# Loads of the attention sent at the entries into TensorE's instruction blocks

## The chip, the cores and the metric

One Trainium2 chip, one core of it. A core has five engines that run their own instruction streams: TensorE (PE, with its weight loads as PEld), VectorE (DVE), ScalarE (ACT), GpSimd (POOL) and SyncE (SP, which here only starts transfers), and 16 DMA engines. The metric is the device time of one execution in microseconds. The kernel before took 863.31 us (median of three runs, 861.24 to 863.8).

## The reference

Band attention with global rows, then two MLPs over the same tokens.

```
attention, 4 batches x 8 heads, 32 global + 512 local tokens, head size 64:
  out_g = softmax(q_g k_all / 8) v_all                    # global rows see everything
  out_l = softmax([q_l k_g, q_l k_l if |i-j| <= 32] / 8) [v_g, v_l]
x = out as (4 * 544, 512)
x = elu(x @ w_in) @ w_out              # 512 -> 2048 -> 512
h = x @ w2_in;  g = h if h >= 1, 0 if h <= -1, else (h + 1)^2 / 4
return g @ w2_out
```

All in float32; products in the MLPs are made of a high and a low part of each factor, three matmuls for one.

## The kernel before, in words

The attention comes first. Two heads share a tile (a pair; 16 pairs), and the stage runs over 24 units, in groups of three: the local rows of a pair, the global rows of that pair and the next, the local rows of the next pair. Iteration n of the loop (L732) does the scores of unit n (`s` or `sg`), the transposes of the probabilities of unit n-1 (`pt`, `tg`), the output transposes of unit n-2 (`ot`, `tg3`) and the products with v of unit n-1 (`po`, `pog`). From n = 4 on the first weights are split between them (`prep`, six half tiles of raw words, `wraw`), from n = 9 on the first matmuls of the MLP (`up`) are mixed in. About 125 us after the start the MLPs follow (`up` and `dn`), TensorE going from matmul to matmul.

In the attention the instruction order of each engine is the order of the program (`Pinned`). SP's order is its queue: a load that waits holds up all loads behind it. Loads are issued in `arrive(n)` at the end of an iteration. Each pair needs q (272 KB), k (288 KB) and two halves of v (520 KB each), each half tile of words 512 KB. `load` paces v and words: a load waits until all but the newest 3200 words for each partition have landed (`IN_FLIGHT`). q and k have two buffers each, v has six halves, the raw words one. After k has landed GpSimd spreads it (`spread_keys`), and makes small diagonal tiles of q for the global rows (`spread_queries`).

Of the kernel before, what the change touches and what calls it, by code (L numbers as in the profile page):

```python
# [9 lines left out]
F32 = mybir.dt.float32  # L10
# [11 lines left out]
S = SG + SL  # L22
# [3 lines left out]
P = 128  # L26
NPAIR = H // 2
# [26 lines left out]

V_UNTIL = {0: 2, 1: 4, 2: 6, 3: 7, 4: 9, 5: 11}

# [10 lines left out]
def band_attention_then_two_mlps(  # L67
# [35 lines left out]
    acc = {}  # L103

    class Pinned:


        def __init__(self, engine):
            self.engine = engine

        def __getattr__(self, name):
            fn = getattr(self.engine, name)
            return lambda *args, **kw: tc.keep_in_program_order(fn(*args, **kw))  # L113

# [10 lines left out]

    def load(out, src, words, paced=True):
# [12 lines left out]
        loads.append((ins, words))  # L139
# [21 lines left out]

    def prep(wraw_p, wtmp_p, layer, f, c0, n, raw_tag="wraw"):

# [7 lines left out]
        raw = wraw_p.tile([P, n], U64, tag=raw_tag, name="wraw")  # L171
        load(raw, (w1, w2)[layer][f][:, c0:c0 + n], 2 * n)
        words = raw.bitcast(U32).rearrange("p (n two) -> p n two", two=2)
# [203 lines left out]
    with ExitStack() as actx:  # L377
# [6 lines left out]
        sp_p = apool("sp", 4, side="right")  # L384
        raw_p = apool("raw", 2, side="right")
        win_p = apool("win", 4, side="right")
# [20 lines left out]

        def load_qk(b, hp):
            q_sb = raw_p.tile([P, S], F32, tag="q", name="q_sb")
            k_sb = raw_p.tile([P, KPAD + NSUB * 64], F32, tag="k", name="k_sb")  # L410
            both = [(q_sb, qT), (k_sb[:, 0:KPAD], kT)]
            for sb, dram in both if b + hp else both[::-1]:
                load(sb, dram[b, hp], sb.shape[1], paced=False)
            loaded[b, hp] = [q_sb, k_sb, diag[(NPAIR * b + hp) % 4]]

        def load_v(b, hp, es=(0, 1)):
            for e in es:
                v_sb = win_p.tile([P, 2, half * VW + 2], F32, tag="v", name="v_sb", bufs=6)
                v_sb = v_sb[:, :, 0:half * VW]
                src = vwin[b, hp, :, half * e:half * e + half]  # L420
                src = src.rearrange("p (s a) h v -> p s (a h v)", s=2)
                load(v_sb, src, half * 2 * VW)
                v_sb = v_sb.rearrange("p s (a h v) -> p s a h v", a=half // 2, h=2)
                landed.setdefault((b, hp), []).append(v_sb)
# [233 lines left out]
        for _ in range(WARM_UP):  # L658
            eng.tensor.matmul(idle, zeros[:, 0:P], zeros)
        load_qk(*pairs[0])  # L660
        eng.scalar.dma_start(mask_sb, mask)
        eng.scalar.dma_start(eye_sb, eye)
        load_qk(*pairs[1])
        load_v(*pairs[0])
# [11 lines left out]
        def early_weights():  # L676

            for part in parts:
                for _ in range(3):
                    next(part, None)  # L680
                    yield
# [17 lines left out]

        parts = [prep(g_p, wtmp_p, 0, *part, raw_tag="wraw") for part in halves]  # L700
        sent = iter(parts)
        weights, ups = early_weights(), early_ups()
# [7 lines left out]

        def arrive(n):
# [19 lines left out]
        live, first = {}, {}  # L731
        for n in range(len(units) + 2):  # L732
            if n > UP_AT:
                next(ups, None)
            part(n, "scores")
            part(n - 2, "norm")
            part(n - 1, "turn")
# [12 lines left out]
            arrive(n)  # L750
            if n == len(units):
# [144 lines left out]
```

## Time and profile before

| | |
|---|---|
| median of three runs | 863.31 us |
| profiled execution, its own time | 864.74 us |
| its span, first to last instruction | 862.9 us |
| PE, DVE, ACT busy | 844.9, 581.4, 431.7 us |
| mean granted TensorE clock | 0.996 |
| attention stage, to the first `dn` | about 129 us |

Times in the views are microseconds from the span's start. A wait in brackets is idle time just before the row, and what ended it; "issue" means that the profile shows nothing that the engine waited for. The queue q1 carries the loads, q8 the instructions of TensorE. A share of the DMA is the mean busy share of the 16 DMA engines.

### The profile page before, as it was taken

How to read it: one execution, taken by the hardware profiler on the slowest of the kernel's cores; microseconds unless marked ns; L12 is line 12 of the kernel's file. 1: busy time of each engine (PE TensorE's matmuls, PEld its weight loads, DVE VectorE, ACT ScalarE, POOL GpSimd, SP SyncE). 2: the span in 40 equal slices, each digit the busy share in tenths (PEclk: the TensorE clock that was granted, in tenths of full speed). 3: DMA queues.
4: the chain of work that ended last, by engine and by line, in shares of the span. 5: the costliest groups of instructions: out<-in, count | busy, mean ns of one | idle time of the engine just before them, and what ended most of it. 6: DMA issues, size and time to landing. Idle time of an engine off the chain costs nothing.

```text
span 862.9 us, 14906 instructions
## 1 busy us (share of the span) xinstructions
PE 844.9 (98%) x6138; PEld 694.0 (80%) x6138; DVE 581.4 (67%) x1130; ACT 431.7 (50%) x755; POOL 28.2 (3%) x66
## 2 busy tenths in 40 slices
PE   8799899999999999999999999999999999999998
PEld 5677778888888888888888888888888888888886
DVE  4689765879527964834399896368759754845455
ACT  5678674666335543533357564456435333433332
POOL 2122200000000000000000000000000000000000
PEclk9999999999999999999999999999999999999999
DMA  8888722222101210200022112012101200000014
GB/s 265 288 275 266 222 78 98 97 98 98 50 0 49 98 49 0 98 1 1 0 71 77 49 50 97 1 40 93 63 1 58 90 0 1 1 1 0 2 62 146
DMA packets 23124, 65.45 MB, mean 76 GB/s; under 512 B 3984, under 2 KB 4240, under 8 KB 19344
## 3 DMA queue, kind: packets, MB, share of 16 engines
q1 hardware_dynamic: 22768, 64.23, 21.8%
q8 instruction: 48, 0.79, 0.4%
q10 hardware_dynamic: 288, 0.26, 0.1%
q14 instruction: 20, 0.16, 0.1%
HBM read 60.03 MB, written 4.46 MB: 75 GB/s over the span
## 4 chain that ended last, share of the span: by engine, by line
PE 93%; DMA 3%; DVE 2%; issue 1%; ACT 1%; SPq 0%
PE dn L320 40%; PE up L247 39%; PE up L244 3%; PE dn L337 3%; PE up L113 2%; PE po L113 2%; DMA k_sb<-in_kT 1%; PE pt L113 1%; PE s L113 1%; PE sg L113 1%; PE tg L113 1%; DMA wraw<-in_w 1%; DVE top L113 1%; DMA v_sb<-in_vwin 1%; PE ot L113 1%
## 5 line engine op out<-in xcount | busy, mean ns | idle before, releaser
L320 PE MATMUL dn<-gh,wh 128*128 128x512 f32 x506 | 196.9, 389 | 0.0
L320 PE MATMUL dn<-gl,wh 128*128 128x512 f32 x506 | 196.8, 389 | 0.0
L320 PE MATMUL dn<-gh,wl 128*128 128x512 f32 x506 | 196.3, 390 | 0.0
L247 PE MATMUL up<-xh,wl 128*128 128x512 f32 x492 | 192.5, 391 | 0.0
L247 PE MATMUL up<-xl,wh 128*128 128x512 f32 x492 | 191.6, 389 | 0.0
L247 PE MATMUL up<-xh,wh 128*128 128x512 f32 x492 | 191.6, 389 | 0.0
L278 ACT ACTIVATE gh<-g 128x512 fp32r<-128x512 f32 x123 | 77.7, 632 | 118.7 <-DVE g L267 71.8
L297 DVE TENSOR_TENSOR acc<-dn,acc 128x512 f32<-128x512 f32 x128 | 84.9, 685 | 48.7 <-PE dn L320 48.4
L320 PEld LDWEIGHTS dn<-gl,wh 128*128 128x128 f32 x506 | 95.0, 188 | 19.9
L282 DVE TENSOR_TENSOR gl<-g,gh 128x512 fp32r<-128x512 f32 x123 | 84.6, 689 | 38.9 <-ACT gh L278 37.8
L320 PEld LDWEIGHTS dn<-gh,wh 128*128 128x128 f32 x506 | 95.0, 188 | 19.4
L320 PEld LDWEIGHTS dn<-gh,wl 128*128 128x128 f32 x506 | 95.0, 188 | 19.4
L247 PEld LDWEIGHTS up<-xh,wh 128*128 128x128 f32 x492 | 92.3, 188 | 19.3
L247 PEld LDWEIGHTS up<-xl,wh 128*128 128x128 f32 x492 | 92.4, 188 | 18.8
L247 PEld LDWEIGHTS up<-xh,wl 128*128 128x128 f32 x492 | 92.4, 188 | 18.7
L258 ACT ACTIVATE g<-up,half_sb 128x512 f32<-128x512 f32 (+1 forms) x69 | 47.0, 681 | 113.6 <-PE up L247 104.8
L266 DVE SCALAR_TENSOR_TENSOR g<-g 128x512 f32<-128x512 f32 (+1 forms) x69 | 46.9, 680 | 59.4 <-ACT g L258 59.3
L264 DVE SCALAR_TENSOR_TENSOR g<-up,g 128x512 f32<-128x512 f32 x64 | 43.4, 679 | 62.5 <-ACT g L255 62.5
L253 ACT ACTIVATE g<-up 128x512 f32<-128x512 f32 x64 | 37.8, 590 | 86.2 <-PE up L247 80.6
L267 DVE TENSOR_TENSOR g<-g,e 128x512 f32<-128x512 f32 (+1 forms) x69 | 46.9, 680 | 3.6
L180 ACT ACTIVATE top<-wraw 128x1024 f32<-128x1024 f32 x29 | 33.7, 1163 | 29.2 <-DMA wraw<-in_w 24.1
L255 ACT ACTIVATE g<-g,one_sb 128x512 f32<-128x512 f32 x64 | 45.8, 716 | 1.8
(112 smaller groups left out, 923.6 us busy)
## 6 DMA issues: line engine op xcount, KB each, us to landing
wraw<-in_w SPq DMA_DIRECT2D x29, 1024.0 KB, 4.8
v_sb<-in_vwin SPq DMA_DIRECT2D x32, 520.0 KB, 5.3
k_sb<-in_kT SPq DMA_DIRECT2D x16, 288.0 KB, 3.9
q_sb<-in_qT SPq DMA_DIRECT2D x16, 272.0 KB, 5.2
outT<-acc SPq DMA_DIRECT2D x16, 256.0 KB, 2.1
wraw<-in_w SPq DMA_DIRECT2D x6, 512.0 KB, 4.6
outT<-acc_rows SPq DMA_DIRECT2D x4, 64.0 KB, 2.2
mask_sb<-in_mask ACTq DMA_DIRECT2D x1, 192.0 KB, 3.4
```

What stands on the lines that cost most here:

```text
L113: return lambda *args, **kw: tc.keep_in_program_order(fn(*args, **kw))
L247: eng.tensor.matmul(self.ps, w, x, start=k == 0, stop=k == 3 * KT - 1)
L253: eng.scalar.activation(self.g, self.ps, AF.Exp)
L255: eng.scalar.activation(self.g, self.g, AF.Relu, bias=one_sb, scale=-1.0)
L258: eng.scalar.activation(self.g, self.ps, AF.Relu, bias=half_sb, scale=0.5)
L264: eng.vector.scalar_tensor_tensor(g, self.ps, 0.0, g, ALU.max, ALU.subtract)
L266: eng.vector.scalar_tensor_tensor(g, g, 1.0, g, ALU.min, ALU.mult)
L267: eng.vector.tensor_tensor(g, g, self.e, ALU.add)
L278: eng.scalar.activation(self.gh, self.g, AF.Copy)
L282: eng.vector.tensor_tensor(self.gl, self.g, self.gh.bitcast(F32), ALU.subtract)
L297: eng.vector.tensor_tensor(a, ps, a, ALU.add)
L320: eng.tensor.matmul(banks[d], w[:, d * P:(d + 1) * P], g, start=f == fs[0] and k == 0, stop=f == fs[-1] and k == 2,)
```

## The change

Loads from the third pair's q and k and the second pair's v on are no longer issued where the program's loop comes by. The wrapper of TensorE counts what it issues, 4 for a matmul of float32 and 2 for another matmul or a transpose, and when the count passes 186 + 250.5 k it calls `by_blocks` with that matmul. That picks up to three items (q and k of a pair, a half of v, a half tile of words), in the order in which they will be needed, as far as buffers allow, and each waits for that matmul to be done. The pacing by words in flight doesn't apply to these v loads; for the words `load` still has it. q and k have three buffers; the third k lies in the accumulator of the MLP's first batch, which the attention doesn't use.

```
+AT_ONCE = 3
+FIRST_BLOCK, BLOCK = 186, 250.5
...
+            def issue(*args, **kw):
+                ins = tc.keep_in_program_order(fn(*args, **kw))
+                if name in ("matmul", "transpose"):
+                    self.issued += 4 if name == "matmul" and args[1].dtype == F32 else 2
+                    if self.issued > FIRST_BLOCK + self.block * BLOCK:
+                        self.block += 1
+                        at_block(ins)
+                return ins
...
+    def load(out, src, words, paced=True, behind=None):
         ins = eng.sync.dma_start(out, src)
+        if behind is not None:
+            tc.add_manual_dep(ins.ins, behind.ins.name, LANDED, reason="loads by blocks")
...
+        qs = [raw_p.tile([P, S], F32, name=f"q_sb{i}") for i in range(3)]
+        ks = [raw_p.tile([P, k_cols], F32, name=f"k_sb{i}") for i in range(2)]
+        ks.append(acc[0].rearrange("p d n -> p (d n)")[:, 0:k_cols])
...
+        def by_blocks(ins):
+            for _ in range(AT_ONCE):
+                found = []
+                p = now["qk"]
+                if p < len(pairs) and now["n"] >= 3 * ((p - 3) // 2) + 1 + (p - 3) % 2:
+                    found.append((3 * (p // 2) + p % 2 - 1, 0, send_qk))
+                p = len(pairs) - (len(ahead) + 1) // 2
+                if ahead and 2 * len(pairs) - len(ahead) < now["until"]:
+                    found.append((3 * (p // 2) + p % 2 + 1, 1, send_v))
+                if now["free"] and len(parts) < len(halves):
+                    found.append((3 * len(parts) + 3, 2, send_words))
+                if found:
+                    min(found, key=lambda item: item[:2])[2](ins)
...
-            if r == 1 and p + 1 < len(pairs):
-                load_qk(*pairs[p + 1])
-            elif r == 2 and p + 2 < len(pairs):
-                load_qk(*pairs[p + 2])
-            elif r == 0 and g:
-                next(next(sent, iter([0])))
-            while ahead and len(ahead) > 2 * len(pairs) - V_UNTIL.get(n, 4 * g + (4, 6, 7)[r]):
-                load_v(*ahead.pop(0))
+            now["until"] = 4 * g + (6, 6, 8)[r]
+            while now["qk"] < len(pairs) and now["qk"] <= p + (r == 2):
+                send_qk()
...
+            if n > 3 and n % 3 == 2:
+                now["free"] = True
```

SP's queue at the start of the attention, first as it was, from the third pair's q on; the numbers of buffers tell loads apart, DMAHW are semaphores of earlier loads.

```order
L113 DMA q_sb_286<-in_qT 128x544 [waits DMAHW0_49,DMAHW1_49,PE_49,Pool_49]
L113 DMA k_sb_287<-in_kT 128x576 [waits DVE_49,PE_49,Activation_49]
L113 DMA v_sb_290<-in_vwin 128x2x520 [waits DMAHW6_49,DMAHW2_49]
L113 DMA v_sb_292<-in_vwin 128x2x520 [waits DMAHW7_49,DMAHW3_49]
L113 DMA q_sb_398<-in_qT 128x544 [waits DMAHW4_49,PE_49,Pool_49]
L113 DMA k_sb_399<-in_kT 128x576 [waits DMAHW5_49,Pool_49]
L113 DMA v_sb_402<-in_vwin 128x2x520 [waits DMAHW2_49]
L113 DMA v_sb_404<-in_vwin 128x2x520 [waits DMAHW3_49]
L113 DMA wraw_519<-in_w1 128x512 [waits DMAHW5_49,DMAHW0_49]
```

The same loads on SP in the changed kernel. The first row and the fifth begin a burst: they wait for a matmul (PE), and the others stand behind them in the queue.

```order
L126 DMA q_sb2_127<-in_qT 128x544 [waits DMAHW0_49,PE_49]
L126 DMA acc0_90<-in_kT 128x576 [waits DMAHW1_49]
L126 DMA v_sb_244<-in_vwin 128x2x520 [waits DMAHW2_49]
L126 DMA v_sb_246<-in_vwin 128x2x520 [waits DMAHW3_49]
L126 DMA q_sb0_125<-in_qT 128x544 [waits DMAHW4_49,PE_49,Pool_49]
L126 DMA k_sb0_128<-in_kT 128x576 [waits DMAHW5_49,DVE_49,Activation_49]
L126 DMA wraw_330<-in_w1 128x512 [waits DMAHW6_49,DMAHW2_49]
L126 DMA v_sb_335<-in_vwin 128x2x520 [waits DMAHW7_49]
L126 DMA v_sb_442<-in_vwin 128x2x520 [waits DMAHW0_49,PE_49]
```

The first words move ahead of the third pair's v, and each burst has one wait for TensorE at its head where every load had waits of its own. Later, in the repeating part of the stage, SP has this order now (from the eighth pair on):

```order
L113 DMA q_sb_1275<-in_qT 128x544
L113 DMA k_sb_1276<-in_kT 128x576
L113 DMA v_sb_1279<-in_vwin 128x2x520
L113 DMA v_sb_1281<-in_vwin 128x2x520
L113 DMA q_sb_1394<-in_qT 128x544
L113 DMA k_sb_1395<-in_kT 128x576
L113 DMA v_sb_1398<-in_vwin 128x2x520
L113 DMA wraw_1525<-in_w1 128x512
L113 DMA v_sb_1530<-in_vwin 128x2x520
```

And in the changed kernel, one group's three bursts, of 1600, 1592 and 520 KB:

```order
L126 DMA q_sb0_125<-in_qT 128x544
L126 DMA k_sb0_128<-in_kT 128x576
L126 DMA v_sb_1276<-in_vwin 128x2x520
L126 DMA v_sb_1278<-in_vwin 128x2x520
L126 DMA wraw_1391<-in_w1 128x512
L126 DMA q_sb1_126<-in_qT 128x544
L126 DMA k_sb1_129<-in_kT 128x576
L126 DMA v_sb_1398<-in_vwin 128x2x520
L126 DMA v_sb_1510<-in_vwin 128x2x520
```

The words head the second burst, ahead of q and k; the third holds a half of v alone. TensorE's order is the same in both kernels but for the names of the buffers.

## Rows read from the trace of the kernel before

**Rows 1.** The page: engines' busy time; the instruction queue (packets, MB, share).

```profile
PE 844.9 (98%) x6138; PEld 694.0 (80%) x6138; DVE 581.4 (67%) x1130; ACT 431.7 (50%) x755; POOL 28.2 (3%) x66
...
q8 instruction: 48, 0.79, 0.4%
```

**Rows 2.** Waits of TensorE: us in total, times, longest us.

```profile
PE s L113 <- issue: 2.8, 3, 1.8
PE pog L113 <- issue: 2.7, 2, 1.4
...
PE po L113 <- issue: 2.4, 2, 1.9
...
PE sg L113 <- DMA k_sb<-in_kT: 0.4, 1, 0.4
...
PE pog L113 <- DMA v_sb<-in_vwin: 0.2, 1, 0.2
```

**Rows 3.** Timeline of TensorE: start, us, what, count, idle before.

```profile
10.14 1.09 PE L113 MATMUL pt<-eye_sb,sn 128*128 128x128 f32 x8
...
16.36 1.21 PE L113 MATMUL pog<-v_sb,pgT 96*32 96x65 f32 x48
...
19.96 1.16 PE L113 MATMUL po<-v_sb,pT 128*32 128x65 f32 x64
21.05 1.22 PE L113 MATMUL sg<-k_sb,diag 128*64 128x272 f32 x12
...
29.97 0.65 PE L113 MATMUL pog<-v_sb,pgT 96*32 96x65 f32 x14 [1.26 <-issue]
...
33.82 0.42 PE L113 MATMUL po<-v_sb,pT 128*32 128x65 f32 x13
36.15 1.32 PE L113 MATMUL po<-v_sb,pT 128*32 128x65 f32 x51 [1.90 <-issue]
37.39 2.19 PE L113 MATMUL sg<-k_sb,diag 128*64 128x272 f32 x12
```

**Rows 4.** DMA, from 29.97 to 33.7 us, then 33.7 to 34.8.

```profile
q1 hardware_dynamic: 607, 1.21, 93.4%
...
q8 instruction: 1, 0.02, 5.8%
```

**Rows 5.** TensorE at 117.57, and DMA from 118 to 119.5 (tenths in 40 slices).

```profile
117.57 0.39 PE L113 MATMUL up<-xh,wl 128*128 128x512 f32 x1
...
DMA  0009000000000000000000000000000000000000
```

**Rows 6.** Windows: busy us (instructions) of PE, PEld, DVE, ACT, POOL; PEclk, DMA share, GB/s.

```profile
25.00:30.00 5.00, 3.38 (x126) 2.55 (x115) 4.70 (x24) 3.43 (x9) 1.14 (x2) 1.00 0.96 313
...
35.00:40.00 5.00, 3.85 (x66) 2.96 (x66) 2.57 (x6) 2.21 (x7) 1.20 (x2) 0.66 0.80 235
...
90.00:95.00 5.00, 4.72 (x104) 3.75 (x111) 2.79 (x18) 2.51 (x7) 0.42 (x2) 0.66 0.41 119
```

**Rows 7.** Windows by groups of three units: n = 3 to 5, 6 to 8, 12 to 14.

```profile
17.49:31.39 13.90, 11.62 (x357) 9.19 (x350) 11.25 (x53) 12.21 (x35) 3.56 (x8) 1.00 0.92 301
31.39:48.35 16.96, 13.25 (x358) 10.17 (x351) 12.00 (x55) 10.49 (x29) 3.21 (x8) 0.90 0.87 279
62.00:76.69 14.69, 13.99 (x368) 11.10 (x363) 13.38 (x57) 12.34 (x33) 3.73 (x8) 1.00 0.82 262
```

**Rows 8.** The tile q_sb from 90 to 93 us: one load and its matmuls.

```profile
L113 PE MATMUL s<-k_sb,q_sb x38: 266/269/293, 90.3 to 90.9; 64*32 64x128 f32 x38
...
L113 SPq DMA_DIRECT2D q_sb<-in_qT x1: 341/341/341, 91.2 to 91.2; - x1
...
DMA to landing us min/median/max: 2.9/2.9/2.9
```

**Rows 9.** Timeline of SP from 5 to 12 us.

```profile
7.04 0.34 SPq L113 DMA_DIRECT2D q_sb<-in_qT  x1
...
10.40 1.62 SPq L113 DMA_DIRECT2D v_sb<-in_vwin  x2
```

More of the change, by code (lines that the diff above doesn't have):

```diff
@@ L103, in band_attention_then_two_mlps, with at_block @@
     acc = {}
+    on_block = []
+    def at_block(ins):
+        for what in on_block:
+            what(ins)
     class Pinned:
@@ L109, in __init__ @@
             self.engine = engine
+            self.issued = 0
+            self.block = 0
         def __getattr__(self, name):
             fn = getattr(self.engine, name)
-            return lambda *args, **kw: tc.keep_in_program_order(fn(*args, **kw))
+            def issue(*args, **kw):
[6 more added lines that the diff above has]
+                return ins
+            return issue
     class Engines:
@@ L160, in place, with prep @@
         return ring[ci % 2], f - chunks[ci][1][0]
-    def prep(wraw_p, wtmp_p, layer, f, c0, n, raw_tag="wraw"):
+    def prep(wraw_p, wtmp_p, layer, f, c0, n, raw_tag="wraw", behind=None):
         tiles, at = place(layer, f)
@@ L171, in prep @@
         raw = wraw_p.tile([P, n], U64, tag=raw_tag, name="wraw")
-        load(raw, (w1, w2)[layer][f][:, c0:c0 + n], 2 * n)
+        load(raw, (w1, w2)[layer][f][:, c0:c0 + n], 2 * n, behind=behind)
         words = raw.bitcast(U32).rearrange("p (n two) -> p n two", two=2)
@@ L384, in band_attention_then_two_mlps @@
         sp_p = apool("sp", 4, side="right")
-        raw_p = apool("raw", 2, side="right")
+        raw_p = apool("raw", 1, side="right")
         win_p = apool("win", 4, side="right")
@@ L406, in band_attention_then_two_mlps, with load_qk, load_v @@
         half = NSUB // 2
-        def load_qk(b, hp):
-            q_sb = raw_p.tile([P, S], F32, tag="q", name="q_sb")
-            k_sb = raw_p.tile([P, KPAD + NSUB * 64], F32, tag="k", name="k_sb")
+        k_cols = KPAD + NSUB * 64
+        qs = [raw_p.tile([P, S], F32, name=f"q_sb{i}") for i in range(3)]
+        ks = [raw_p.tile([P, k_cols], F32, name=f"k_sb{i}") for i in range(2)]
+        ks.append(acc[0].rearrange("p d n -> p (d n)")[:, 0:k_cols])
+        def load_qk(p, behind=None):
+            b, hp = pairs[p]
+            q_sb, k_sb = qs[p % 3], ks[p % 3]
             both = [(q_sb, qT), (k_sb[:, 0:KPAD], kT)]
[L412 to L416, printed above, removed]
+            for sb, dram in both if p else both[::-1]:
+                load(sb, dram[b, hp], sb.shape[1], paced=False, behind=behind)
+            loaded[b, hp] = [q_sb, k_sb, diag[p % 4]]
+        def load_v(b, hp, es=(0, 1), behind=None):
             for e in es:
@@ L421, in load_v @@
                 src = src.rearrange("p (s a) h v -> p s (a h v)", s=2)
-                load(v_sb, src, half * 2 * VW)
+                load(v_sb, src, half * 2 * VW, paced=behind is None, behind=behind)
                 v_sb = v_sb.rearrange("p s (a h v) -> p s a h v", a=half // 2, h=2)
@@ L659, in band_attention_then_two_mlps @@
             eng.tensor.matmul(idle, zeros[:, 0:P], zeros)
-        load_qk(*pairs[0])
+        load_qk(0)
         eng.scalar.dma_start(mask_sb, mask)
         eng.scalar.dma_start(eye_sb, eye)
-        load_qk(*pairs[1])
+        load_qk(1)
         load_v(*pairs[0])
@@ L676, in early_weights @@
         def early_weights():
-            for part in parts:
+            for i in range(len(halves)):
+                while len(parts) <= i:
+                    send_words()
                 for _ in range(3):
-                    next(part, None)
+                    next(parts[i], None)
                     yield
@@ L698, in early_ups @@
                 u.low()
-        parts = [prep(g_p, wtmp_p, 0, *part, raw_tag="wraw") for part in halves]
-        sent = iter(parts)
+        parts, now = [], dict(n=0, until=4, free=True, qk=2)
         weights, ups = early_weights(), early_ups()
@@ L709, in part, with send_qk, send_v, send_words @@
                 live[n][name]()
-        def arrive(n):
+        def send_qk(behind=None):
+            load_qk(now["qk"], behind)
+            now["qk"] += 1
+        def send_v(behind=None):
+            load_v(*ahead.pop(0), behind=behind)
+        def send_words(behind=None):
+            parts.append(prep(g_p, wtmp_p, 0, *halves[len(parts)], behind=behind))
+            next(parts[-1])
+            now["free"] = False
+        def by_blocks(ins):
[11 more added lines that the diff above has]
+                    min(found, key=lambda item: item[:2])[2](ins)
+        def arrive(n, place):
             g, r = divmod(n, 3)
             p = 2 * g + 1
-            if r == 1 and p + 1 < len(pairs):
-                load_qk(*pairs[p + 1])
-            elif r == 2 and p + 2 < len(pairs):
-                load_qk(*pairs[p + 2])
-            elif r == 0 and g:
-                next(next(sent, iter([0])))
-            while ahead and len(ahead) > 2 * len(pairs) - V_UNTIL.get(n, 4 * g + (4, 6, 7)[r]):
-                load_v(*ahead.pop(0))
+            now["n"] = n
+            if place == 0:
+                return
+            now["until"] = 4 * g + (6, 6, 8)[r]
+            while now["qk"] < len(pairs) and now["qk"] <= p + (r == 2):
+                send_qk()
             if r == 0 and g and p < len(pairs):
@@ L731, in band_attention_then_two_mlps @@
         live, first = {}, {}
+        on_block.append(by_blocks)
         for n in range(len(units) + 2):
@@ L735, in band_attention_then_two_mlps @@
             part(n, "scores")
+            arrive(n, 0)
             part(n - 2, "norm")
@@ L748, in band_attention_then_two_mlps @@
             part(n - 1, "values")
-            arrive(n)
+            arrive(n, 1)
             if n == len(units):
```

2 lines of the change are left out of this document (removed).

## The prediction

> **What bounds the kernel now.** I read the page's busy row first: TensorE is busy for 98% of the 862.9 us span [rows 1]. So a change to loads can only win what TensorE loses, and the view to ask next is its waits. Nearly all of them lie in the first 125 us, the attention stage: 7.9 us, in seven waits, go to "issue", which is time in which TensorE waited for nothing that the profile shows; the data loads stopped it for 0.6 us in all [rows 2]. The timeline shows where the issue waits stand: inside a run of equal matmuls, for instance between record 13 and record 51 of one `po` [rows 3]. Counting records between two of them gives a multiple of 125 each time (36 `pog` from 29.97 us on, 64 `s`, 8 `pt`, 4 `tg`, 13 `po` to the next), and 125 records are 250 of the change's units. 48 instruction packets serve 6138 matmuls and as many weight loads [rows 1], 256 instructions each. So these are entries into blocks of instructions that have not arrived.
>
> Next the DMA view in two narrow windows [rows 4]. TensorE entered a block at 29.97 us. Until 33.7 us no instruction packet ran, though the data queue kept its 16 engines 93% busy; then one packet ran within 1.1 us, and TensorE went on at 36.15 [rows 3]. The fetch for the block after is thus due when a block is entered; it stood 3.7 us behind data, took about 1.0 (5.8% of 16 engines in 1.1 us), and 1.4 us later the block could start. By the same count a block is entered at the `up` of 117.57 us; no data moved then, and the packet ran in the fourth fortieth of the window from 118.0, some 0.6 us after the entry [rows 5]. An undisturbed fetch therefore needs about 0.8 + 1.0 + 1.4 = 3.2 us; blocks here last 2.6 to 8 us.
>
> The clock says what the longest stalls cost besides: after the 1.90 and the 1.82 us waits TensorE was granted 0.66 on the mean of the 5 us window, part of it at 1.2 GHz instead of 2.4 [rows 6]. `sg` x12 took 2.19 us there against 1.22 at 21.05, and the 51 `po` before it 1.32 where 51 x 0.017 are 0.87 [rows 3]: 1.4 us, and the second place alike, 2.8 us together.
>
> **The change, part by part.** It removes the pacing and makes each load wait for the first matmul of a block, up to three items at once (q and k of a pair count as one). The engines' instruction order is the same but for SP and the buffers' names, so TensorE's work is untouched.
>
> What could go: 7.9 us of issue waits. Each is counted from the modelled end of the last matmul, which lies about 0.2 us after its successor would have begun (13 `po` take 0.42 us on their own, where 64 take 1.16, or 0.017 for each further one [rows 3]), so seven stalls cost 7.9 + 7 x 0.2 = 9.3. With the clock: 12.1 us.
>
> What comes back as fetch stalls: this is the largest unknown, and I work it out block by block. With the stalls taken out, the blocks from the first entry (the last of eight `pt` begun at 10.14 [rows 3], at 10.96 us) on last 2.6, 3.7, 5.6, 3.8, 4.1, 4.4, 4.1, 4.5, 6.1, 3.9, 4.9, 6.1, 3.8, 5.0, 6.1, 3.6, 5.8, 4.9, 3.6 us; three make one group of three units, and 3.9 + 4.9 + 6.1 fits the 14.69 us of such a group [rows 7]. SP started a load at 91.24, 0.4 us after the last matmul it waited for [rows 8], and that load of 272 KB, alone in the queue, landed 2.9 us after [rows 8]. At the full rate (313 GB/s at a share of 0.96, so 326 [rows 6]) its bytes take 0.85, so a burst's bytes flow from about 2.0 us behind the entry. The bursts, in KB: 1600, 1592, 1600, 1600, 1592, then 1040, 1600, 1072, 1040, and then the repeating 1600, 1592, 520. A full one takes 5.0 us, so it ends 7.0 us behind its entry, later than all blocks but one end. The rule I carry from block to block: the fetch starts 0.8 us after its entry or when the bursts of earlier blocks are through, whichever is later; the next block starts 2.4 us after that, or when the matmuls are done. It gives stalls of 0.6, 0.2, 0, 0.6, 1.0, 0.55, 0, 0.8 in the first eight blocks, then 0.65 once in each group of three, and 1.45 at the nineteenth: 6.5 us. None reaches 1.8, so I cost the clock at nothing. The same rule with 313 GB/s gives 8.8 and with 340 gives 4.6 (single windows go from 294, 235 at a share of 0.80 [rows 6], to 347, 1.21 MB in 3.73 us at 0.934 [rows 4]); I keep 326, the busiest window's.
>
> What is late at the start: now the third pair's q goes out at 7.04 us and the second pair's v at 10.40 [rows 9]. Afterwards these and k wait for the first block entry, so q starts at 11.4 and its bytes at 13.0; 560 KB and then two v halves of 520 end at 14.8, 16.4 and 18.1, and land some 0.45 later. Global rows of the first two heads' pairs (`pog`, 16.36 us now [rows 3]) would be ready at 15.85, wait 1.0 us for the first half of v, and, 0.6 us of work later, 1.1 for the second: 2.1 us. A bound from the other side is 0.5, if the bytes start with the 10.40 rows' delay; nothing below, since no load is earlier. Behind these matmuls stand all of TensorE's later ones. Word loads come earlier than now, which hides them fully; they do wait for VectorE to release the one word buffer, and the loads behind that word load on SP then start up to 1.5 us late. I cost that at nothing, since most bursts find the queue still full; without that cover it is one more stall of up to 1.5.
>
> What VectorE keeps: in the group from 17.49 us on VectorE is busy for 11.25 us and ScalarE for 12.21, TensorE for 11.62, and in the next VectorE for 12.00 [rows 7]. Without stalls these groups cannot be shorter than 12.2 and 12.0 us, where TensorE would come to some 11.7 each; they keep 0.8 us of the gain. The third buffers for q and k and the k buffer laid into the accumulator add no instruction; the accumulator's first real write comes after the attention.
>
> Sum: -12.1 + 6.5 + 2.1 + 0.8 = -2.7 us, against the profiled execution's 864.74 (span 862.9 and 1.8 around it), so 862.0. That execution is 0.17% above the median of 863.31; set against the median the forecast is **860.6 us**.
>
> **Rivals.** *First, the fetch finds the way free.* Bursts issued back to back may move at 347 GB/s or more, and every entry that finds the engines empty has its fetch before the new data. For it: the 340 case already leaves only 4.6, and the DMA share of a late group is 0.82 [rows 7]. Against it: the early groups need 3.8 MB in 12 us. Stalls of 3, `pog` late by 1.5 and VectorE's 0.8 give 5.3 - 12.1 = -6.8, so 856.5.
> A rule speaks for this side. The Trainium skill (DMA: Bandwidth & Descriptors, Queues, rings and completion order) says that a DMA engine takes turns between its queues packet by packet; by that a fetch waits for about one packet, and only the first entry's 0.6 would be left, some 854.7. The trace disagrees: 3.7 us with no instruction packet among 607 of data [rows 4]; so I give it no more than this rival's chance.
>
> *Second, on the other side: the burst's first load overtakes the fetch.* It holds if a busy DMA engine serves in order of arrival and the load's descriptors get there first: SP needs 0.4 + 0.34 us to have issued it, the fetch is seen 0.6 us after its entry at best. Then each fetch due in a busy queue also waits for a load of 272 to 520 KB, 0.85 to 1.6 us, and the same rule gives 15.3 us of stalls, four of them over 2 us. Time 15.3 + 2.1 + 0.8 - 12.1 = +6.1, so 869.4. For it: how closely those times lie together. Against it: the fetch has a lead of some 0.6 us over the first bytes. It decides from the point where first bytes flow less than about 1 us after an entry.
>
> *Third, the stalls only move.* At 300 to 313 GB/s the rule leaves 8.8 or more, and every stall over 1.8 would bring the slow clock back: -12.1 + 8.8 + 2.1 + 0.8 = -0.4, so 862.9. The same time comes out if the change does not do what it says because its count of units drifts from the true entries: loads then go out at fixed but arbitrary places, and stalls stay as frequent.
>
> **Chances.** Forecast 0.43 (its own range 858 to 863), free way 0.16, overtaking 0.20, stalls that move 0.21. A measurement of this kernel tells a change from none at about 0.3%, 2.6 us. The forecast lies just at that edge: some 0.25 of its 0.43 is faster, 0.17 the same, 0.01 slower; free way is all faster; moved stalls are the same but for 0.03 slower; overtaking is slower but for 0.01. Faster 0.41, same 0.36, slower 0.23. The range from 855.5 to 868.5 leaves out the far end of the free way and half of the overtaking.
>
> **What would show it.** Right: issue waits of 5 to 8 us, more of them (eight to twelve) and none over 1.5; no granted clock under 1.0 before 125 us; a wait of `pog` for v_sb of 1 to 2 us near 16 us; stage end (the first `dn`) some 3 us earlier. Wrong: issue waits over 10 us, or several over 1.8 with the clock at 1.2 GHz behind them (overtaking); under 4 us (free way); new waits of TensorE for k_sb or POOL after 20 us, which I have at zero; or a change in the span after 130 us, which nothing here touches.

## The result, and the profile after

The changed kernel takes 867.6 us (median of 7, 866.65 to 871.55) where the kernel before takes 862.98 on the same chip: 1.0061 of it, 95% interval 1.0043 to 1.0080. It is slower by 0.6%; the prediction, 860.6 us, had the wrong sign, though its wide range (855.5 to 868.5) still holds 867.6. The profiled execution took 867.51 us (span 865.7), 2.8 more than that of before.

TensorE's waits after, in the columns of [rows 2]:

```profile
PE tg L126 <- DVE og L126: 3.9, 5, 0.8
PE po L126 <- issue: 3.8, 4, 1.8
PE pog L126 <- DMA v_sb<-in_vwin: 3.0, 2, 2.1
...
PE pt L126 <- ACT wh L126: 0.7, 1, 0.7
PE pog L126 <- issue: 0.6, 1, 0.6
PE po L126 <- DMA v_sb<-in_vwin: 0.5, 1, 0.5
...
PE s L126 <- issue: 0.2, 1, 0.2
```

The issue waits fell from 7.9 us to 4.6; the waits for `v_sb` rose from 0.2 to 3.5, and those of `tg` for VectorE's `og` from 2.5 to 3.9. The waits for v come at the start, where the timeline of after (start, us, what, count, idle before) has:

```profile
14.65 0.30 PE L126 MATMUL pog<-v_sb,pgT 96*32 96x65 f32 x2
15.85 0.77 PE L126 MATMUL pog<-v_sb,pgT 96*32 96x65 f32 x24 [0.90 <-DMA v_sb<-in_vwin]
18.76 1.02 PE L126 MATMUL pog<-v_sb,pgT 64*32 64x65 f32 x22 [2.15 <-DMA v_sb<-in_vwin]
19.72 1.96 PE L126 MATMUL s<-acc,q_sb 64*32 64x128 f32 x64
21.60 1.97 PE L126 MATMUL pt<-eye_sb,sn 128*128 128x128 f32 x8
23.50 0.48 PE L126 MATMUL tg<-eye_sb,og 128*64 128x64 f32 x4
23.92 1.75 PE L126 MATMUL po<-v_sb,pT 128*32 128x65 f32 x64
...
33.85 1.16 PE L126 MATMUL s<-k_sb,q_sb 64*32 64x128 f32 x64
```

The 48 `pog` that ran in one piece before [rows 3] wait twice, 3.05 us. And then the same 64 `s` take 1.96 us that take 1.16 at 33.85; 8 `pt` take 1.97 where 1.09 was the duration before, 64 `po` 1.75 for 1.16 [rows 3]. The windows of after, in the columns of [rows 6], show the clock that goes with it:

```profile
15.00:20.00 5.00, 2.00 (x62) 1.40 (x70) 0.99 (x4) 2.67 (x9) 1.52 (x6) 0.85 1.00 345
20.00:25.00 5.00, 5.00 (x116) 4.17 (x104) 2.40 (x20) 1.99 (x6) 1.24 (x3) 0.50 0.70 233
25.00:30.00 5.00, 4.83 (x138) 3.98 (x136) 2.92 (x8) 4.20 (x12) 1.69 (x4) 0.97 0.64 214
...
45.00:50.00 5.00, 4.33 (x166) 3.45 (x171) 4.58 (x23) 3.25 (x10) 2.02 (x6) 1.00 0.70 213
...
90.00:95.00 5.00, 4.93 (x159) 3.69 (x161) 4.16 (x19) 3.28 (x8) 0.34 (x2) 1.00 0.25 72
```

TensorE was busy for 2.0 of the 5 us to 20; then the granted clock is 0.50, TensorE at 1.2 GHz, until a little behind 25. In the window of 90 us it is 1.00, where before had 0.66 [rows 6], and it is 1.00 behind the longest issue wait of after, too (1.77 us at 44.59, shown below). When the same matmuls start in both timelines:

| | before, us | after, us | after minus before |
|---|---|---|---|
| first `po` | 11.48 | 10.45 | -1.0 |
| `s` behind the `pog` of 16 us | 17.49 | 19.72 | +2.2 |
| the `sg` after it | 21.05 | 25.60 | +4.6 |
| `s` of the group from n = 6 | 31.39 | 33.85 | +2.5 |
| `s` of the group from n = 9 | 48.35 | 49.42 | +1.1 |
| `s` of the group from n = 12 | 62.00 | 64.47 | +2.5 |
| `s` at n = 17 | 87.81 | 91.97 | +4.2 |
| `s` at n = 18 | 94.90 | 95.87 | +1.0 |
| last 64 `po` of the attention | 128.26 | 130.89 | +2.6 |
| last matmul | 858.83 | 861.46 | +2.6 |

Up to 26 us the change loses 5.6 us. Where before had its stalls of 30, 36, 48 and 88 to 94 us, it gives back 2.1, 3.2, 0.8 and 3.2; what lies between takes 7.4 again.

One new wait shows how a fetch is now held up. TensorE entered a block at 37.31 us, 13 `po` behind the start of the first row below; then the DMA view from 37.31 to 42.1 us, and from 42.1 to 43.2:

```profile
36.88 1.42 PE L126 MATMUL po<-v_sb,pT 128*32 128x65 f32 x64
...
42.07 0.75 PE L126 MATMUL po<-v_sb,pT 128*32 128x65 f32 x34 [0.55 <-DMA v_sb<-in_vwin]
44.59 0.43 PE L126 MATMUL po<-v_sb,pT 128*32 128x65 f32 x14 [1.77 <-issue]
```

```profile
q1 hardware_dynamic: 562, 1.34, 90.4%
```

```profile
q1 hardware_dynamic: 215, 0.42, 99.2%
q8 instruction: 1, 0.02, 5.3%
```

562 data packets ran before the one instruction packet, 4.8 us behind the entry. An entry is here, as in the prediction, the first matmul of the new block. Read in this way for the first 20 entries, the delay from entry to packet is 0.6 to 1.1 us where the queue was all but empty (9.93 to 10.52, 60.92 to 61.95, 76.74 to 77.83, 92.67 to 93.77) and 3.4 to 4.8 in a busy one (64.52, 70.30, 80.41, 86.30, 96.27, 112.26). Their sum is about 51 us; before it was about 49. So the rule moved the delays to other entries and made them no shorter in sum.

The last of these is not a case of bytes put out earlier alone. The last matmul of the old block began at 111.85 us, the first of the new one at 112.26. (Where a wait stands at an entry, the expectations below count from the last matmul of the old block: 111.85 for 112.26, 85.59 for 86.30, 48.09 for 48.95.) The DMA row from 111.85 to 116.7 us (40 slices of 0.12 us, tenths) and what SyncE gave out:

```profile
DMA  2222121100000068468899999699899999999999
```

```profile
112.58 0.88 SPq L126 DMA_DIRECT2D v_sb<-in_vwin  x2
```

The engines stood empty for 0.7 us from 112.8 on, and the fetch due at 112.26 did not run; it ran at 116.70, behind two loads given out 0.3 and 0.7 us after its entry. Overtaking exists, at least at this entry.

### The profile page after: what moved, and what is told of

Read it like the earlier page. It is cut to its first block, busy times and chain, and to the rows that moved or that the text cites. A ratio compares the mean times of both kernels' runs of the same rounds, so it can differ in the third digit from the quotient of the medians.

```text
span 865.7 us, 14894 instructions
## 1 busy us (share of the span) xinstructions
PE 845.6 (98%) x6138; PEld 694.4 (80%) x6138; DVE 580.8 (67%) x1130; ACT 431.4 (50%) x755; POOL 28.3 (3%) x66
## 4 chain that ended last, share of the span: by engine, by line
PE 94%; DVE 2%; ACT 1%; DMA 1%; issue 1%; SPq 0%; POOL 0%
PE dn L343 40%; PE up L270 39%; PE up L267 3%; PE dn L360 3%; PE po L126 2%; PE up L126 2%; PE s L126 1%; PE pt L126 1%; DMA v_sb<-in_vwin 1%; PE sg L126 1%; DVE top L126 1%; PE tg L126 1%; PE pog L126 1%; PE dn L126 0%; PE ot L126 0%
## 5 line engine op out<-in xcount | busy, mean ns | idle before, releaser
L343 PEld LDWEIGHTS dn<-gh,wh 128*128 128x128 f32 x506 | 95.0, 188 | 19.5
L282 ACT ACTIVATE e<-up,nhalf_sb 128x512 f32<-128x512 f32 (+1 forms) x69 | 46.6, 676 | 0.3 <-DVE g L290 0.3
```

What stands on the lines that cost most here:

```text
L282: eng.scalar.activation(self.e, self.ps, AF.Relu, bias=nhalf_sb, scale=0.5)
L343: eng.tensor.matmul(banks[d], w[:, d * P:(d + 1) * P], g, start=f == fs[0] and k == 0, stop=f == fs[-1] and k == 2,)
```

## The experiments

Each was timed in five rounds beside the kernel before on its chip, but for the last two; ratios are to the kernel before, with 95% intervals.

**The start cured in two ways.** `e1_early_first` loads q, k of the third pair and v of the second in the preamble, `e5_v1_first` only v.

```diff
         load_v(*pairs[0])
+        load_qk(2)            # e1 alone
+        load_v(*pairs[1])     # both
...
```

> The changed kernel, but the third pair's q and k and the second pair's v are issued right behind the first loads of the program, v paced as in the kernel before; all later loads go out at the block entries as changed. Theory A (the loss is made at the start: the first burst lets the DMA queue run empty, pog waits 3.05 us for v, and the stall brings 6.8 us of the 1.2 GHz clock; the later bursts trade seven long instruction stalls for many short ones and win about 1.9 us): the wait of pog for v_sb under 1 us, no granted clock of 0.5 between 18 and 26 us, the first dn about 5 us earlier than in the changed kernel, time 861.5 to 863, ratio to the kernel before 0.997 to 1.000. Theory B (bursts in the later groups make the loss, the start is made good later by engines that had caught up): less than 2 us won, 866 or more.

Measured: 866.5 us, 1.0036 (1.0013 to 1.0059). No wait for v is left, but its timeline has, at the same place:

```profile
21.94 1.03 PE L126 MATMUL pt<-eye_sb,sn 128*128 128x128 f32 x8 [3.23 <-issue]
...
23.22 1.80 PE L126 MATMUL po<-v_sb,pT 128*32 128x65 f32 x64
```

The fetch due at 14.78 us ran at 19.5, behind 1.55 MB of data, and the slow clock followed (1.80 for 64 `po`). A wait for data had become a wait for instructions. The time is theory B's; that the later groups make the loss, its reason, this does not show.

> The changed kernel with one edit: the two v loads of the second pair go out in the preamble, and nothing else is moved there (e1_early_first had moved q and k of the third pair too, and got a 3.23 us instruction wait at 21.94 us). Theory S (the start lost the time: pog waits 0.90 and 2.15 us for v at 15.85 and 18.76 us, and the slow clock behind it): both waits for v are gone, no instruction wait over 1 us before 30 us, the profiled s, po and pt of 18 to 26 us take their full-clock durations; 861.5 to 863.5 us. Rival F (the bytes of the first 25 us are the same, so whatever is not waited for as v is waited for as instructions): an instruction wait of 2 to 3.5 us somewhere between 13 and 27 us with a stretch of slow clock behind it, and 865.5 to 867.5 us.

Measured: 865.5 us, 1.0033 (1.0018 to 1.0048), the lower edge of rival F's range. The profile, of its quickest execution, is neither expectation's: no wait is for v; the longest of the start is one of 1.7 us for instructions at 15.10, and the granted clock there stays 1.00:

```profile
PE tg L126 <- DVE og L126: 4.2, 5, 1.0
PE s L126 <- issue: 4.1, 3, 1.7
PE po L126 <- issue: 2.6, 4, 0.9
```

By this the late v and its clock cost about half of the 0.6%, as far as two intervals tell that just overlap; the issue waits are 7.3 us again, about those of before.

**Where in the block the bursts start.** Four kernels move the point, with the old or the cured start:

```diff
-FIRST_BLOCK, BLOCK = 186, 250.5
+FIRST_BLOCK, BLOCK = 146, 250.5   # e11, 0.5 us sooner
+FIRST_BLOCK, BLOCK = 226, 250.5   # e7, 0.5 us later
+FIRST_BLOCK, BLOCK = 311, 250.5   # e2, mid-block; e4: e2 with the start of e1
```

> The changed kernel with the first threshold at 311 instead of 186, so that every burst goes out half a block after an entry, long after the instruction fetch of that entry is due. Theory A with overtaking (a fetch that finds the queue busy also waits for loads issued up to 1.2 us behind its entry, as at 111.85 us in the changed kernel, where it ran 4.8 us late behind two loads issued 0.7 and 1.1 us after the entry): the bursts come too late to overtake the fetch of their own block, but a burst of 5 us then ends 7 us behind the middle of a block and stands before the next entry's fetch; delays of 2 to 5 us at most entries, issue waits over 6 us, and the first v another 1.5 us later: 869 to 873. Theory C (alignment with the entries does nothing, only the amount in flight counts): within 2 us of the changed kernel, issue waits as there (4.6 us).

> Both edits: the first loads early as in the first kernel of this set, all others half a block after the entries. Against that kernel it tells what the alignment with the entries is worth, without the loss at the start. Theory A: 2 to 5 us slower than with the entries, issue waits over 6 us. Theory C: within 1.5 us of it.

> The changed kernel with FIRST_BLOCK 226 for 186: every load waits for a matmul about 0.5 us deeper in the block. Theory O (a burst's first loads overtake the fetch of the same entry, as the two loads issued 0.73 and 1.15 us behind the entry at 111.85 us seem to): fetches get ahead of them, instruction waits fall from 4.6 us to under 3, 863.5 to 866 us. Rival Q (only what was in the queue before the entry delays a fetch): delays of fetches the same within 0.5 us, loads land 0.5 us later, so the waits for v and the spill into the next block grow; 867.5 to 871 us.

> The changed kernel with FIRST_BLOCK 146 for 186: every load waits for a matmul about 0.5 us ahead of the entry. Theory Q (a fetch waits for what was put into the queue before it, e7_later_in_block only lost because its loads landed later): the burst now stands ahead of the fetch of its own entry, every entry-to-fetch delay rises to 3.5 us or more, instruction waits above 7 us, while the waits for v shrink; 869 to 873 us. Rival E (sooner is better, since the burst ends sooner ahead of the next entry): fetches at 4 us or less everywhere, instruction waits under 4.6 us, 863 to 866 us.

Measured: sooner 872.1 us, 1.0103 (1.0073 to 1.0133); at the entry 1.0061; later 870.7, 1.0099 (1.0074 to 1.0125); mid-block 876.6, 1.0150 (1.0119 to 1.0181); mid-block with the cured start 872.1, 1.0117 (1.0080 to 1.0154). So the entry is the best of the four points, though its interval still touches those of its two neighbours. Bursts do start at entries: a burst's first load goes out at 10.23 us for the entry at 9.93, at 61.36 for 60.92. Mid-block, theory C falls; theory A has the direction, and both kernels are slower than it said. Later by half a microsecond, four of the six long delays shrink (70.78 us: 2.2, 80.63: 1.1, 96.82: 1.0, 113.21: 1.9), as theory O has it, but others grow (21.90: 3.3), the issue waits are 5.5 us and not under 3, the waits for v 4.2, and the time is rival Q's: fetches come sooner at some entries, and nothing is gained in sum. Sooner, the issue waits are 10.6, as theory Q has it, with the burst ahead of its own fetch, though not every delay grew.

**What all loads of v cost.** `e3_before_no_v` is the kernel before, where from the fourth pair on an old tile of v is used instead of a new load, so it computes with other values:

```diff
+                if p >= 3:
+                    old = landed[pairs[p - 3]][e]
+                    landed.setdefault((b, hp), []).append(old)
+                    continue
```

> The kernel before, but the v of the fourth pair and later isn't loaded: the tiles of the pair three before are used again, so 13.5 MB fewer are moved in the attention and the output is that of other values. It bounds what any schedule of these loads can win. Theory A (fetches stand behind data): no issue wait of TensorE after 20 us, no 0.5 clock, 852 to 854.5, that is 8.5 to 11 us under the kernel before. If the stalls are the fetches' own latency and not the data's doing: issue waits of 4 us or more stay, and the time is above 858.

Measured: 855.6 us, 0.9918 (0.9892 to 0.9944). Of TensorE's waits 2.2 us are for issue, and the granted clock of all six executions was 0.999 or 1.0. So an order of the loads of v can win at most some 0.8%. Behind 20 us the issue waits are 1.0 us where before had 7.1: most of them come with these bytes. Theory A had none left and 852 to 854.5 us; its rival's 858 is farther off. `tg` waits 3.9 us for `og` here too:

```profile
PE tg L113 <- DVE og L113: 3.9, 5, 0.8
...
PE s L113 <- issue: 1.2, 1, 1.2
...
PE po L113 <- issue: 0.8, 1, 0.8
```

**Smaller bursts, and both mends.**

```diff
-AT_ONCE = 3
+AT_ONCE = 2     # e6; e8: with the start of e5
...
+            while ahead and 2 * len(pairs) - len(ahead) < 4 * g + (4, 4, 6)[r]:
+                send_v()
```

> The changed kernel with bursts of at most two loads (AT_ONCE 2); a v load that would come too late is sent by its deadline instead. Theory Q (a fetch waits for the bytes that were put into the queue before its entry, so that what costs is a burst of three that is still running at the next entry, as at 37.31, 48.09 and 85.59 us): the instruction waits of TensorE fall from 4.6 us to 3 or less, the entry-to-fetch delays of 3.4 to 4.8 us become rarer; the start is as late as in the changed kernel or later (v of the second pair), so 864 to 867 us. Rival R (a queue that gets two loads at every entry is busy at every entry, and each fetch stands behind loads): instruction waits above 6 us and 869 us or more.

> e5_v1_first and e6_two_at_once together. Theories S and Q: no wait for v at 15 to 20 us, instruction waits under 3 us in all, at most one stretch of slow clock; 858 to 861 us, below the kernel before. Rival F with R: 866 us or more, with instruction waits above 6 us.

Measured: 864.3 us, 1.0024 (1.0007 to 1.0041), and together 864.6, 1.0029 (1.0013 to 1.0045). `e6` has the lowest median of the changed line and is still not below before. In its one profile (of its longest execution, 868.1 us) the issue waits are 8.5 us, not under 3: the time that theory Q expected came, the reason did not show. Something else shows. The edit's second part sends v by a deadline, and so the second pair's v goes out at 7.88 us, sooner than in the kernel before [rows 9]:

```profile
7.88 1.70 SPq L126 DMA_DIRECT2D v_sb<-in_vwin  x2
```

`pog` does not wait for it, and the granted clock is 1.00 up to 30 us. So `e6` is one more cure of the start. `e8` cures it a second time, gains nothing by that, and lies between its expectations. What smaller bursts are worth by themselves is not shown.

**The word load at the head of a burst.** In the changed kernel it waited on SyncE for VectorE, and the burst behind it:

```diff
-            if n > 3 and n % 3 == 2:
+            if n > 3 and n % 3 == 0:
                 now["free"] = True
```

> The changed kernel with the next load of weight words let out one unit later (n % 3 == 0 for n % 3 == 2). In its trace five of the six word loads stood at the head of a burst and waited there for VectorE's last read of their only buffer (12.3 us in five waits), so that SyncE gave those bursts out 1.6 to 3.4 us behind the entry (36.09, 50.53, 66.47, 82.18, 97.87 us), and the next fetches came 4.84, 1.65, 4.59, 4.84 and 1.96 us behind their entries. Theory H (this head-of-line wait is what spoils the alignment): SyncE's waits for VectorE's top go, the bursts leave within 0.9 us of every entry, instruction waits fall from 4.6 to 3 us or less; the late v at 15 to 20 us stays; 864 to 866 us. Rival B (a burst of three fills the queue into the next block wherever it starts): delays and waits as before, now in the bursts that carry the words; 867 to 869 us.

SyncE's waits (us in total, times, longest), the changed kernel's and then this one's:

```profile
SPq L126 <- DVE top L126: 12.3, 5, 3.8
```

```profile
SPq L126 <- DVE top L126: 2.0, 1, 2.0
```

Most of the wait is gone, but the time is 866.9 us, 1.0045 (1.0025 to 1.0064), between the two expectations, the issue waits are 5.4 us, not 3 or less, and fetches still come 3.5 to 5.7 us late at 46.12, 61.79, 83.88 and 94.72. Theory H falls as the main cause. Rival B's reason, that a burst of three fills the queue into the next block, is argued and not shown: bursts of two had more issue waits (e6). With the start of e5 it is 865.7, 1.0031 (1.0009 to 1.0053), what e5 has alone, as rival B has it; on this one chip the cured start is worth 1.2 us:

> e5_v1_first (v of the second pair in the preamble, 865.5 us) and e9_words_later together. Theory H: instruction waits 4 us or less (7.3 in e5_v1_first's profile), 861 to 863.5 us. Rival B: 864.5 to 866.5 us.

**The two halves of the change apart.** `e12` gives the kernel before the third buffers and keeps its order; `e13` gives the changed kernel two buffers and keeps its rule; `e14` is e13 with the start of e5.

```diff
-            q_sb = raw_p.tile([P, S], F32, tag="q", name="q_sb")     # e12, from before
+            q_sb, k_sb = qs[p % 3], ks[p % 3]
...
-            q_sb, k_sb = qs[p % 3], ks[p % 3]                        # e13, from after
+            q_sb, k_sb = qs[p % 2], ks[p % 2]
...
-                if p < len(pairs) and now["n"] >= 3 * ((p - 3) // 2) + 1 + (p - 3) % 2:
+                if p < len(pairs) and now["n"] >= 3 * ((p - 2) // 2) + 1 + (p - 2) % 2:
```

> The kernel before with the third query and key buffer of the change alone (the third key buffer in acc), its order of loads kept. Theory: a load that had to wait for a buffer was late by less than it waited for others in flight; within 0.3% of the kernel before, with the same stall at 88 us. Rival: q and k go out sooner and stand in front of other fetches; 1 to 3 us either way.

> The other half of the change alone: its rule of blocks and bursts, but two query and key buffers as before (a pair's q and k may go out once the pair two back is read). The third buffers alone, in the order of before, measured 1.0040 [1.0019, 1.0061] of the kernel before (e12_before_three_buffers). If the two halves add (theory P), the rule alone is 1.002 of before, 864 to 866 us, with the late v of the start (3 us at 15 to 20 us) still there. Rival J: the rule needs the third buffers (loads that wait for a buffer hold SyncE's queue up in mid-block), and is as slow as with q and k late: 868 us or more. Rival N: the buffers are nothing inside the rule, 867 to 868 us.

> e13_rule_two_buffers with v of the second pair in the preamble (e5_v1_first had the same with three buffers: 1.0033 [1.0018, 1.0048]). Theory P with S: no wait for v at 15 to 20 us, and the buffers' 0.4% saved: 861 to 863 us, within 0.3% of before. Rivals J and N: 865 to 868 us.

Measured: the buffers alone 866.3 us, 1.0040 (1.0019 to 1.0061); the rule alone 878.8, 1.0183 (1.0154 to 1.0212); with the cured start 877.7, 1.0178 (1.0145 to 1.0211). Both expectations of halves that add fall. Rival J is right for e13, and e14 is slower than any expectation of it. The first waits of e13, and then of e14:

```profile
PE s L126 <- POOL k_sb L126: 9.7, 4, 3.2
PE pog L126 <- DMA v_sb<-in_vwin: 3.1, 2, 1.7
```

```profile
PE s L126 <- POOL k_sb L126: 14.3, 6, 3.0
...
PE s L126 <- issue: 1.1, 2, 0.9
```

With two buffers a pair's q and k can go out only once the pair two back is read, the burst after that is late, and `s` waits for GpSimd's work on k. The issue waits are down to 1.1 us here, and nothing was gained by that, since the data are late. The third buffers alone lose 2.6 us, as their rival allowed (1 to 3 us either way). What SyncE waited for, before and with them:

```profile
SPq L113 <- PE s L113: 23.3, 7, 6.4
...
SPq L113 <- PE pt L113: 13.3, 8, 3.3
SPq L113 <- DMA v_sb<-in_vwin: 10.7, 8, 2.3
```

```profile
SPq L113 <- DMA v_sb<-in_vwin: 31.4, 19, 4.9
...
SPq L113 <- PE pog L113: 14.6, 6, 5.9
...
SPq L113 <- PE pt L113: 1.2, 4, 0.4
...
SPq L113 <- PE s L113: 0.7, 1, 0.7
```

Before, a buffer still in use held loads back until TensorE had come to a certain matmul; `s` and `pt` make 36.6 us of that, 1.9 with the third buffers (`pog` makes 14.6 in their place, for 2.4 before). Now mostly the loads in flight hold them, and they go out as soon as one lands. That this is why it loses I argue from the waits; no run shows it by itself.

**The depth of the queue by itself.**

```diff
-IN_FLIGHT = 3200     # the kernel before
+IN_FLIGHT = 2200
```

> The kernel before with at most 2200 words for 3200 in flight, two loads for three. Theory Q (a fetch of instructions waits for the bytes that stand in the queue at its entry, so the depth of the queue sets the stalls): delays from entry to fetch of at most 3.3 us, TensorE's instruction waits 4 us or less for 7.9; the loads land later, waits for v and k of 1 to 4 us appear in their place; 860 to 864 us. Rival T (16 engines with fewer loads in flight lose throughput, everything lands late): waits for v and k above 6 us, 868 us or more.

Measured: 873.3 us, 1.0116 (1.0090 to 1.0143).

```profile
PE pog L113 <- DMA v_sb<-in_vwin: 4.6, 3, 3.9
PE s L113 <- POOL k_sb L113: 3.6, 3, 1.4
PE po L113 <- issue: 1.9, 2, 0.9
...
PE s L113 <- issue: 1.4, 2, 1.2
```

The issue waits halve, 3.7 us for 7.9 (with 0.4 of `pog`), as theory Q has it, though single delays reach 4.7 us where it allowed 3.3; but data comes late, and more is lost than won, as rival T has it.

**All three mends at once**: start, bursts of two, two buffers.

> All three mends of the changed kernel at once: v of the second pair in the preamble, bursts of at most two loads, two query and key buffers. If the single effects add (e5_v1_first -2.1 us against the changed kernel, e6_two_at_once -3.3, buffers -2.6): 859.5 to 862 us, below before. Rival (they are the same microseconds counted three times, as e8_v1_two showed for the first two): 863.5 to 866 us.

Measured: 878.2 us, 1.0176 (1.0144 to 1.0208). Neither expectation comes out: the late k of the two buffers is there again (13.1 us of `s` behind GpSimd).

**What comes every time.** A second profiled execution each of the changed kernel and of e5.

> The changed kernel, a second profiled execution, to part what comes in every execution from what falls otherwise each time. Theory S: the waits of pog for v at 15 to 20 us (3.05 us in the first) and a stretch of slow clock right behind them are there again; the places of the later instruction waits, and of other slow stretches, may differ. Rival V (the start of the first profile was an accident of that execution): less than 1.5 us of waits for v, no slow clock before 26 us.

The changed kernel took 870.61 us (the kernel before, once beside it, 866.32). Its timeline, and two windows:

```profile
16.32 0.77 PE L126 MATMUL pog<-v_sb,pgT 96*32 96x65 f32 x24 [1.81 <-DMA v_sb<-in_vwin]
18.78 1.02 PE L126 MATMUL pog<-v_sb,pgT 64*32 64x65 f32 x22 [1.69 <-DMA v_sb<-in_vwin]
19.73 1.96 PE L126 MATMUL s<-acc,q_sb 64*32 64x128 f32 x64
...
104.08 1.94 PE L126 MATMUL pt<-eye_sb,sn 128*128 128x128 f32 x8 [3.09 <-issue]
```

```profile
100.00:105.00 5.00, 1.91 (x17) 1.67 (x14) 2.55 (x8) 1.26 (x4) 0.70 (x2) 0.82 0.61 224
105.00:110.00 5.00, 5.00 (x17) 3.98 (x15) 1.72 (x3) 3.11 (x6) 0.91 (x4) 0.50 0.83 263
```

At the `sg` behind it the start is the same to 0.3 us (25.31, 25.60): 3.5 us of waits for v, and the same slow `s`. The profiles of e7 and e9, with nearly the same start, have it too (3.7 and 3.5 us, granted clock 0.54 and 0.73 from 20 to 25 us). Theory S holds. The issue wait of 3.09 us at 104 with its slow clock is new, and large enough to make this execution the longer one. 

> e5_v1_first, a second profiled execution; the first was its quickest run of 12 (863.15 us against a median of 865.49, granted clock 0.999). If the 2.3 us between them are slow clock and instruction waits that fall otherwise each time, an execution near the median shows 1 to 2 stretches of slow clock more or 2 us more of instruction waits, and its s, po and pt durations elsewhere the same. Rival: another wait, of one fixed place, that the quick execution did not have.

This one took 863.59 us, granted clock 1.0, with no wait for v and 6.8 us of issue waits. It too lies below e5's median of 865.49, so it decides nothing, and what the 0.33% of e5 consists of stays open.

## Why the prediction was wrong

| term | predicted | measured in the profile |
|---|---|---|
| stalls of before and their slow clock gone | -12.1 | -12.1, by the way of counting (what is left at their places is in the next row) |
| new fetch stalls | +6.5 | 4.6 + 6 x 0.2 = +5.8 |
| v late | +2.1 | 3.0 + 0.5 = +3.5 |
| slow clock behind new stalls | 0 | +2.7 |
| VectorE | +0.8 | 3.9 - 2.5 = +1.4 |
| sum | -2.7 | +1.3; the spans differ by 2.8 (0.7 more is `pt` behind ScalarE, 0.8 I can't place) |

**The step that failed is "None reaches 1.8, so I cost the clock at nothing".** I asked for the clock only behind the fetch stalls that I had worked out, and not behind the wait for v, which I priced one paragraph later at 1.0 and 1.1 us, one right after the other. They came as 0.90 and 2.15, with 0.77 us of work between, and from 18.4 to 25.3 us the granted clock was 0.51. Price: 0.80 for the 64 `s`, 0.88 for the `pt`, 0.59 for the `po`, 0.14 for `tg`, and 0.3 for 22 `pog` (1.02, where (1.21 - 0.77) / 24 each makes 0.73 with the fixed part): 2.7 us, nearly the 2.8 that I had booked as a gain for the two places of before. That the clock comes with the wait, the profiles of e5 and e6 bear out: no wait of `pog` for v, and a granted clock of 1.00 up to 30 us.

My own numbers could have shown it. With the blocks and bursts that I listed, my rule gives a stall of some 2.4 us at the third entry, not 0.2. The first burst is through 7.0 us behind the first entry, so the third block can start at 9.4; but the second is entered at 3.2 and has 3.7 us of matmuls. The 0.2 comes out only if the 2.1 us of waits for v lie in that same second block, which I did not write. Either way TensorE stands still for 2.3 us or more in one block, over the 1.8 that I took as the mark.

**v late was mis-sized, on TensorE's side.** The second half landed at 18.72 us where I had 18.1 + 0.45. But I had `pog` ready at 15.85 and it was at 14.65: the first `po` started 1.0 us sooner than before, and each microsecond that TensorE is sooner is one more of waiting for the same load. The 0.5 of the 3.5 is a wait at another place (42.07).

**The fetch stalls were right in sum**, 5.8 for 6.5, and not by place, so this is partly luck: the longest, 1.77, stands where I had 0.55, and where I had 1.0 there is none; in the second execution they make 7.0 + 6 x 0.2 = 8.2. Nor is the rule (a fetch waits for the bytes of earlier blocks) the whole: at 112.26 later bytes passed as well, and the fetch due at 12.97 ran at 16.70, while the earlier burst's last load landed at 18.72. One of the seven issue waits that I read from before (0.17 at 42.49) stands 139 records behind the last and is no entry. Of the 1.4 us more for VectorE, 0.8 are in other groups than the two that I named. Right were these: nothing changes in the span after the attention (+2.6 at its last `po` and at the last matmul), and the word loads' delay on SyncE, which came out longer (12.3 us in five waits), is worth little (e9). Of my marks, "eight to twelve" issue waits were six, one over 1.5; the granted clock, the wait for v and the stage end (2.6 us later, not 3 earlier) went against me too.

**The rival that came near in its number, 869.4, came near for another reason.** It wanted issue waits over 10 us by overtaking; overtaking was there, at one entry at least, but the issue waits were 4.6, and e7, in which four of the six long delays shrink, is slower. The turns packet by packet that I weighed there (the Trainium skill, DMA: Bandwidth & Descriptors, Queues, rings and completion order) do not show here as the wait for one packet, but the trace speaks less clearly against them than I wrote. A packet of the profile is mostly one row of a load (2080 to 4096 bytes); the 562 are some 35 for each of 16 engines, and how many packets in the Trainium skill's sense these make no run shows. Crossing into a block is "mostly hidden", says the Trainium skill (Runtime: NRT & Kernel Launch, Instruction fetch mechanics). Of the first 20 entries 14 have no issue wait in either kernel, which agrees; the other six cost 7.7 us before and 4.6 after.

**The medians differ by 4.6 us, the profiled pair by 2.8.** The pair has a mean granted clock of 0.996 in either kernel. Over the 7 timed executions of the changed kernel it is 0.9949, over 86 of the kernel before, beside the experiments, 0.9972. That is (0.9972 - 0.9949) / 0.5 x 865 = 4.0 us more at 1.2 GHz; at 2.7 us for the 6.9 of the profile, an estimate of 1.6 us. The second execution shows such a stretch at a place of its own.

**Shown, and not shown.** Shown: the late v and the slow clock behind it, in each profile with this start. Kernels with the rule at the entries and three buffers take 1.0024 to 1.0036 where this v goes out sooner (e1, e5, e6, e8, e10), 1.0061 and 1.0045 (e9) where it does not; the intervals overlap, so that the worth of the start is some 1 to 2.5 us and not known better. Shown too: that the third buffers alone cost 0.40%, the rule without them 1.83%, and that the parts do not add. Argued: that new issue waits (7.3 us in e5's profile for 4.6) take part of what the cured start gives. Not shown: where the last 0.33% of e5 is lost. Executions of the kernel before range over some 11 us (858.5 to 870.1), and two profiles of the changed kernel differ in where fetches come late and the clock falls, so single profiles cannot part 3 us into places.

## What to carry to other kernels

When loads are moved, follow the first ones: at the start nothing is buffered, a late burst becomes a wait at once, and a second price comes behind it in clock. Ask for the clock behind every wait that the sum adds, and add up waits that follow one another closely. Where data and instructions share the DMA engines, moving the loads moves the fetch delays about. Issue waits as such are not the aim: later or fewer loads in flight cut them too (e14, e15), and late data cost more; only fewer bytes (e3) cut waits and time together. And when an edit has two parts, ask which of them helped: the deadline in e6 had cured the start.

## What the runs showed of the hardware

A fetch of instructions ran 0.6 to 1.1 us behind its entry when the queue was all but empty, and up to 4.8 us behind it in a busy one (6.5 in the second execution, at 95.06 us). Third buffers alone, with no instruction added, cost 0.40%. And the granted clock differs between executions of one program: 0.992 to 1.0 over 86 of the kernel before, 0.999 or 1.0 in all six of e3, which moves less data.
